# Another order for the opening of a fused attention and Hyena kernel: fp32 loads turned by TensorE, a second batch cast into SBUF, and the filter's spectrum moved into that batch

## The chip, the cores and the metric

The kernel runs on one core of one Trainium2 chip. Time is device time in microseconds (us) for the whole call; most executions of one kernel agree within a few tenths of a per cent.

## The reference

Batch 8, 8 heads, sequence 576, head width 64, 128 random features. The first part is linear attention with cos/sin features, the second a gated FFT convolution.

```python
def phi(x):                                   # attention, per batch and head
    proj = einsum('bhsd,md->bhsm', x, omega)
    return concatenate([cos(proj), sin(proj)], -1) / sqrt(m)
kv  = einsum('bhsm,bhsd->bhmd', phi(k), v);   z = phi(k).sum(axis=2)
num = einsum('bhsm,bhmd->bhsd', phi(q), kv);  den = einsum('bhsm,bhm->bhs', phi(q), z)
x   = (num / den), heads side by side         # (8, 576, 512)
x1, x2, x3 = split(x @ w_proj, 3)             # Hyena part
y   = x1 * irfft(rfft(x2) * rfft(filter_fft)) * x3
out = y @ w_out
```

## The kernel before

For each batch the program issues four `pair(b, hp)` steps of attention (two heads each), interleaved with four `hyena(b - 1, hp)` steps of the batch before. The names matter in the profile: `tk`, `tq` are transposed k and q in PSUM, `kT`, `qT` their copies; `thk`, `thq`, `tht` are projections onto omega; `angk`, `angq`, `angt` angles; `kf`, `qf`, `kft` the cos/sin features; `vh`, `vl` the fp16 high and low parts of v; `kv`, `nd` the attention matmuls; `tx`, `xT` the transposed attention output; `x2p`, `xg` the projections, `yp`, `yg` the spectrum of the input and its product, `xc` the inverse transform, `op` the last projection; `ff` the folded filter and `hps`, `hpi`, `hpm` its spectrum.

```python
def turns(self, th, name):          # one feature: DVE, then GpSimd, then ScalarE's Sin
    t = self.ft.tile([128, 2, w], I32, name=f"ang{name}", tag="ang", bufs=2)
    nc.vector.tensor_scalar(t[:, 0], th, TO_PHASE, None, ALU.mult)
    nc.gpsimd.tensor_scalar(t[:, 1], t[:, 0], 1.0, TURN / 4, ALU.mult, ALU.add)
...
def v_split(self, b, hp):
    nc.scalar.copy(vh, vp)
    nc.gpsimd.tensor_tensor(self.vl[hp], vp, vh, ALU.subtract)
...
def spectrum(self, b):
    self.yg = [mo.tile([128, 2, DM], F32R, name=f"yg{b}_{g}", tag=f"yg{g}") for g in range(2)]
    ...
        nc.gpsimd.tensor_tensor(self.yg[g], t[0], t[1], ALU.add)
...
def run(self):
    self.omega_load()
    self.loads(0)        # k, q of batch 0 cast to fp16 by GpSimd's DMA ring, turned by TensorE
    self.loads(1)        # k, q of batch 1 cast into DRAM, then two DMA transposes (kD -> kT, qD -> qT)
    self.in_weights(); self.buffers()
    self.front(0, 0)
    self.v_split_tails(0)
    for b in range(B + 1):
        for hp in range(4):
            if b < B: self.pair(b, hp)
            if b:     self.hyena(b - 1, hp)
        if b == 0:
            self.filter_spectrum(self.fold_filter())   # fold on DVE, 17 matmuls, 10 evacuations on ScalarE

def pair(self, b, hp):              # front(): k features, v split and q features of the next pair
    if hp < 3: self.front(b, hp + 1)
    elif b + 1 < B: self.front(b + 1, 0)
    ...
    self.kv(b, hp); self.attend(b, hp); ...
```

## Time and profile before

| | before |
|---|---|
| time, median of 3 runs | 432.19 us (431.9 to 434.46) |
| profiled span, mean TensorE clock | 432.9 us, 0.933 |
| busy: PE, DVE, ACT, POOL | 79%, 67%, 55%, 52% |
| x2p of batches 0, 1, 2 starts at | 77.3, 125.6, 173.7 us |

The average shares hide the structure. Up to x2p of batch 0 the core waits for data; from there on each batch takes 47 to 48 us with TensorE dense. (In the timeline x2p of batch 0 starts at 77.27; the chain's entry of 77.49 in the prediction begins where its predecessor ends.)

### The profile page before, as it was taken

The numbers are of one execution on the slowest core, as the hardware profiler recorded it, in microseconds if no ns is written. First come the engines' busy times: TensorE is split into PE (matmuls) and PEld (weight loads), VectorE is DVE, ScalarE is ACT, GpSimd is POOL, SyncE is SP. The second block draws the span as 40 slices with busy tenths as digits, with TensorE's granted clock in tenths as the row PEclk, the third lists the DMA queues.
The fourth block names the chain that finished last, engine by engine and source line by source line (L and its number), as shares of the span: only waits on it lengthen the run. The fifth ranks groups of instructions, "written<-read, shape, count | busy, mean of one in ns | idle before, by whom it ended". The sixth has DMA issues, their size and how long they took to land.

```text
span 432.9 us, 8680 instructions
## 1 busy us (share of the span) xinstructions
PE 340.5 (79%) x3550; PEld 230.4 (53%) x3550; DVE 290.7 (67%) x530; ACT 239.3 (55%) x308; POOL 227.0 (52%) x209
## 2 busy tenths in 40 slices
PE   0277555998779869996989869986899698888982
PEld 0155423666446655565556755666466555673560
DVE  3256963597946888497849786688849784863640
ACT  4056834845766448833884458644883388222432
POOL 7076711378632946477545855294637453423360
PEclk9999956899889989999799969998999979999998
DMA  9999999205940197109930595019510002001203
GB/s 206 204 206 204 286 246 175 49 3 58 235 143 6 10 167 222 43 2 119 226 95 2 62 182 183 14 11 176 108 38 2 2 28 83 2 2 51 59 2 109
DMA packets 76152, 43.50 MB, mean 100 GB/s; under 512 B 43473, under 2 KB 69585, under 8 KB 76113
## 3 DMA queue, kind: packets, MB, share of 16 engines
q1 hardware_dynamic: 52608, 30.52, 30.0%
q0 software_dynamic: 23504, 12.44, 21.5%
q8 instruction: 28, 0.46, 0.5%
q14 instruction: 12, 0.09, 0.1%
HBM read 36.80 MB, written 17.69 MB: 126 GB/s over the span
## 4 chain that ended last, share of the span: by engine, by line
PE 44%; DMA 13%; ACT 12%; DVE 12%; POOL 9%; issue 7%; SPq 2%; POOLq 0%; ACTq 0%; DVEq 0%
PE xg L112 9%; PE kv L420 7%; DMA f<-in_moe_filter_fft_dram 6%; PE xc L112 6%; PE op L112 5%; PE x2p L112 5%; ACT qf L404 4%; ACT kf L382 3%; PE yp L112 3%; DMA out_dram<-o 3%; DMA qa<-in_q_dram 3%; POOL yT L523 3%; PE nd L437 3%; DVE tc L484 3%; ACT o L536 2%
## 5 line engine op out<-in xcount | busy, mean ns | idle before, releaser
L404 ACT ACTIVATE qf<-angq 128x1728 f16<-128x1728 int16 (+1 forms) x48 | 70.4, 1480 | 28.4 <-PE nd L437 20.5
L382 ACT ACTIVATE kf<-angk 128x2048 f16<-128x2048 int16 x32 | 61.1, 1910 | 20.9 <-POOL angk L347 19.0
L112 PE MATMUL xg<-xT,wp 128*128 128x288 f16 x512 | 71.4, 286 | 1.0 <-DVE tc L484 0.3
L347 POOL TENSOR_SCALAR angk<-angk 128x1024 int32<-128x1024 int32 x32 | 33.5, 1046 | 64.7 <-DVE angk L346 64.0
L346 DVE TENSOR_SCALAR angq<-thq 128x864 int32<-128x864 f32 (+1 forms) x48 | 45.6, 952 | 31.4 <-ACT qf L404 20.3
L347 POOL TENSOR_SCALAR angq<-angq 128x864 int32<-128x864 int32 (+1 forms) x48 | 43.2, 900 | 34.5 <-DVE angq L346 33.9
L112 PEld LDWEIGHTS <-wp 128*128 128x128 f16 x512 | 49.3, 98 | 20.2 <-issue 4.2
L485 POOL TENSOR_TENSOR yg<-tc,tc 128x1024 fp32r<-128x1024 f32 x16 | 37.4, 2359 | 36.9 <-DVE tc L484 36.9
L523 POOL TENSOR_TENSOR yT<-w,cv 128x576 f16<-128x576 f32 x32 | 45.7, 1436 | 20.3 <-DVE cv L522 13.2
L503 DVE TENSOR_TENSOR w<-xg,w 128x288 f32<-128x288 f32 x64 | 27.7, 452 | 36.3 <-ACT w L501 18.5
L333 POOL TENSOR_TENSOR vl<-vf,vh 128x512 f16<-128x512 f32 x32 | 36.9, 1155 | 26.7 <-ACT vh L332 26.6
L420 PEld LDWEIGHTS <-kf 128*128 128x128 f16 x1024 | 44.0, 101 | 9.7 <-issue 5.5
L501 ACT ACTIVATE w<-xg 128x288 f32<-128x288 f32 x64 | 24.4, 406 | 38.5 <-PE xg L112 37.9
L112 PE MATMUL op<-wo,yT 128*128 128x512 f16 (+1 forms) x160 | 40.6, 390 | 3.4 <-POOL yT L523 3.4
L346 DVE TENSOR_SCALAR angk<-thk 128x1024 int32<-128x1024 f32 x32 | 39.0, 1218 | 6.3 <-ACT qf L404 5.3
L112 PE MATMUL x2p<-wp,eo 128*128 128x512 f16 x160 | 38.1, 395 | 5.1 <-ACT o L536 4.4
L420 PE MATMUL kv<-vh,kf 128*128 128x65 f16 x512 | 38.8, 199 | 3.6 <-ACT kf L382 1.9
L437 PE MATMUL nd<-kvz,qf 128*128 128x65 f16 x640 | 27.5, 200 | 16.3 <-DVE kvz L425 14.6
L112 PE MATMUL xc<-inv,yg 128*128 128x288 f32 x128 | 35.2, 368 | 5.4 <-ACT w L501 4.6
L437 PEld LDWEIGHTS <-qf 128*128 128x128 f16 x640 | 25.5, 102 | 23.4 <-issue 16.9
L420 PE MATMUL kv<-vl,kf 128*128 128x64 f16 x512 | 37.3, 197 | 0.0
L402 PE MATMUL thq<-qT,om 128*128 128x512 f16 (+1 forms) x96 | 28.4, 378 | 10.9 <-DVE angk L346 6.1
(88 smaller groups left out, 639.6 us busy)
## 6 DMA issues: line engine op xcount, KB each, us to landing
vf<-in_v_dram SPq DMA_DIRECT2D x8, 1024.0 KB, 7.2
qD<-in_q_dram POOLq DMA_DIRECT2D x7, 576.0 KB, 8.7
kD<-in_k_dram POOLq DMA_DIRECT2D x7, 512.0 KB, 6.1
out_dram<-o SPq DMA_DIRECT2D x8, 256.0 KB, 3.0
out_dram<-o SPq DMA_DIRECT2D x8, 224.0 KB, 2.4
wp<-in_moe_w_proj_dram POOLq DMA_DIRECT2D x1, 1536.0 KB, 23.2
out_dram<-o SPq DMA_DIRECT2D x8, 192.0 KB, 3.2
out_dram<-o SPq DMA_DIRECT2D x8, 160.0 KB, 2.1
```

The source lines that it names most:

```text
L112: nc.tensor.matmul(outap, l, r, start=(i == 0), stop=(i == n - 1))
L333: nc.gpsimd.tensor_tensor(self.vl[hp], vp, vh, ALU.subtract)
L346: self.nc.vector.tensor_scalar(t[:, 0], th, TO_PHASE, None, ALU.mult)
L347: self.pool_mark = self.nc.gpsimd.tensor_scalar(t[:, 1], t[:, 0], 1.0, TURN / 4, ALU.mult, ALU.add)
L382: self.marks["k", b, hp] = nc.scalar.activation(kf.rearrange("p t a r m -> p t (a r m)"), ang, AF.Sin, scale=TO_ANGLE)
L402: nc.tensor.matmul(th[:, lo:hi], self.om2[:, r], qT[:, lo:hi], start=True, stop=True)
L404: nc.scalar.activation(self.qf[b][:, :, h0 : h0 + n, r], ang.rearrange("p t (h j) -> p t h j", h=n), AF.Sin, scale=TO_ANGLE,)
L420: nc.tensor.matmul(ps[:, hh, t, : 1 + D] if i < 5 else ps[:, hh, t, :D], l, r_, start=(i == 0), stop=(i == len(terms) - 1),)
L437: nc.tensor.matmul(ps[:, c], qfh[:, t, SOFF[c] : SOFF[c] + 128], kvz[:, hh, t], start=(t == 0), stop=(t == 1),)
L485: nc.gpsimd.tensor_tensor(self.yg[g], t[0], t[1], ALU.add)
L503: nc.vector.tensor_tensor(w[:, ns], ps, w[:, ns], ALU.mult)
L523: nc.gpsimd.tensor_tensor(self.yT[b][:, dc], self.w.pop((b, dc)).rearrange("p a s -> p (a s)"), cv.rearrange("p c z i -> p (c z i)"), ALU. ...
```

## The change

Its intent is to get the first batches going earlier. Batch 0's k, q and v come as plain fp32 through one ring, in the order of use, and TensorE transposes them in fp32. Batch 1's k and q are cast straight into SBUF, into the buffers that `yg` uses later, and TensorE turns them, instead of the way through DRAM. The filter loads no longer wait, and its fold and spectrum move from between batches 0 and 1 into batch 1's loop. (Two smaller parts are not in the cut below: the last filter tile gets other buffers, and the fold is held behind the last attention step of batch 0 instead of the one before.)

```diff
     def run(self):
...
         self.omega_load()
-        self.loads(0)
-        self.loads(1)
-        self.in_weights()
+        self.first_loads()                 # k, q, v of batch 0: nc.sync, FP32, in order of use
         self.buffers()
         self.front(0, 0)
+        with self.tc.issue_after(self.pool_marks["k", 0, 0].ins):
+            self.second_loads()            # k, q of batch 1: nc.gpsimd, cast to FP16 in SBUF
+            self.v_loads(1)
         self.v_split_tails(0)
         for b in range(B + 1):
             for hp in range(4):
                 if b < B:
                     self.pair(b, hp)
+                if b == 1 and hp == 0:
+                    self.fold_filter()
+                if b == 1 and hp == 1:
+                    self.filter_spectrum()
                 if b:
                     self.hyena(b - 1, hp)
-            if b == 0:
-                self.filter_spectrum(self.fold_filter())
...
+    def second_loads(self):
+        ka = mo.tile([128, H, 4 * D], FP16, name="ka1", tag="yg0")
+        qa = mo.tile([128, H, 4 * D], FP16, name="qa1", tag="yg1")
...
     def k_features(self, b, hp):
...
-        if b == 0:
-            self.first_k(blocks, [...], f"tk{hp}")
+        if b < 2:
+            self.first_k(b, hp)
...
-        self.late(nc.sync.dma_start(self.fwd, dr_fwd.ap()), self.marks["k", 0, 1])
+        nc.sync.dma_start(self.fwd, dr_fwd.ap())
...
-                    ld = nc.sync.dma_start(f[p + at : p + at + m], every4[BLOCKS[blk], i : i + m])
-                    self.late(ld, self.marks["k", 0, 1])
+                    nc.sync.dma_start(f[p + at : p + at + m], every4[BLOCKS[blk], i : i + m])
```

More of the change, by code (lines that the diff above doesn't have):

```diff
@@ L39 @@
 QW = 4 * S
-FTAG = ["tc0", "tc1", "tc1", "tc0", "tc0"]
+FTAG = [("tc0", 2), ("tc1", 2), ("tc1", 2), ("tc0", 2), ("xT", 2)]
 QGROUPS = [(0, 3), (3, 3), (6, 2)]
@@ L143, in omega_load @@
         nc, cst = self.nc, self.cst
-        ident = nc.inline_tensor(np.eye(128, dtype=np.float16), name="identc")
+        ident = nc.inline_tensor(np.eye(128, dtype=np.float32), name="identc")
+        self.ident32 = self.mo.tile([128, 128], FP32, name="ident32", tag="cv", bufs=2)
+        nc.sync.dma_start(self.ident32, ident.ap())
+        om = self.mo.tile([128, 64], FP32, name="om", tag="osb", bufs=2)
+        nc.sync.dma_start(om, self.omega)
         self.ident = cst.tile([128, 128], FP16, name="ident", tag="ident")
-        nc.sync.dma_start(self.ident, ident.ap())
-        om16 = cst.tile([128, 64], FP16, name="om16", tag="om16")
-        nc.gpsimd.dma_start(om16, self.omega)
+        nc.vector.tensor_copy(self.ident, self.ident32)
         self.om2 = cst.tile([128, 2, 128], FP16, name="om2", tag="om2")
         nc.vector.memset(self.om2, 0.0)
-        ps = self.bank([128, 128], "omps", FP16)
-        nc.tensor.transpose(ps[:64, :128], om16, self.ident)
+        ps = self.bank([128, 128], "omps")
+        nc.tensor.transpose(ps[:64, :128], om, self.ident32)
         nc.vector.tensor_copy(self.om2[:64, 0], ps[:64, :128])
@@ L174, in weights @@
         with self.tc.issue_after(self.pool_marks["k", 0, 1].ins):
+            self.in_weights()
             nc.gpsimd.dma_start(self.inv, dr_inv.ap())
@@ L191, in filter_loads @@
         for c in range(NC):
-            f = mo.tile([128, 2, DM], FP32, name=f"f{c}", tag=FTAG[c], bufs=2)
+            f = mo.tile([128, 2, DM], FP32, name=f"f{c}", tag=FTAG[c][0], bufs=FTAG[c][1])
             for p, _, lo, n in _filter_rows(c):
                 for blk, i, m, at in _pieces(lo, n, EB):
-                    ld = nc.sync.dma_start(f[p + at : p + at + m], every4[BLOCKS[blk], i : i + m])
-                    self.late(ld, self.marks["k", 0, 1])
+                    nc.sync.dma_start(f[p + at : p + at + m], every4[BLOCKS[blk], i : i + m])
             self.fl.append(f)
@@ L200, in fold_filter @@
         nc, mo = self.nc, self.mo
-        ff = mo.tile([128, NC, DM], FP16, name="ff", tag="x2")
-        with self.tc.issue_after(self.marks["strip", 0, 2].ins):
+        self.ff = ff = mo.tile([128, NC, DM], FP16, name="ff", tag="yT")
+        with self.tc.issue_after(self.marks["strip", 0, 3].ins):
             nc.vector.memset(ff[:, 2], 0.0)
@@ L209, in fold_filter, with filter_spectrum @@
                     )
-        return ff
-    def filter_spectrum(self, ff):
-        nc, cst, fwd = self.nc, self.cst, self.fwd
+    def filter_spectrum(self):
+        nc, cst, fwd, ff = self.nc, self.cst, self.fwd, self.ff
         self.hre = [cst.tile([128, 2, DM], FP16, name=f"hre{g}", tag=f"hre{g}") for g in range(2)]
@@ L249, in loads, with v_tiles @@
     def loads(self, b):
-        nc, raw = self.nc, self.raw
+        self.v_loads(b)
+        self.turned_loads(b)
+    def v_tiles(self, b):
+        raw = self.raw
         vf = raw.tile([128, H, 4, D], FP32, name=f"vf{b}", tag="vf", bufs=2)
@@ L253, in loads @@
         self.vf[b] = vf, vft
-        nc.sync.dma_start(
-            vf.rearrange("p h r d -> p h (r d)"),
-            self.v[b, :, :512, :].rearrange("h (p r) d -> p h (r d)", r=4),
-        )
-        self.tails(nc.sync, vft, self.v, b)
-        self.kT[b] = raw.tile([128, 18, 128], FP16, name=f"kT{b}", tag="kT")
-        self.qT[b] = raw.tile([128, 2 * H, QB], FP16, name=f"qT{b}", tag="qT")
-        if b == 0:
-            self.first_loads()
-        else:
-            self.turned_loads(b)
+        return vf, vft
@@ new lines, in v_loads, with turned_tiles, fours @@
+    def v_loads(self, b, eng=None):
+        nc = self.nc
+        vf, vft = self.v_tiles(b)
+        nc.sync.dma_start(vf.rearrange("p h r d -> p h (r d)"), self.fours(self.v, b, 0, H))
+        self.tails(nc.sync, vft, self.v, b)
+    def turned_tiles(self, b):
+        self.kT[b] = self.raw.tile([128, 18, 128], FP16, name=f"kT{b}", tag="kT")
+        self.qT[b] = self.raw.tile([128, 2 * H, QB], FP16, name=f"qT{b}", tag="qT")
+    def fours(self, src, b, h0, n):
+        return src[b, h0 : h0 + n, :512, :].rearrange("h (p r) d -> p h (r d)", r=4)
@@ L266, in first_loads @@
     def first_loads(self):
         nc, mo = self.nc, self.mo
-        self.ktl = mo.tile([128, 4, D], FP16, name="ktl", tag="od", bufs=2)
-        self.ka = mo.tile([128, H, 4 * D], FP16, name="ka", tag="tc0", bufs=2)
-        self.qa = mo.tile([128, H, 4 * D], FP16, name="qa", tag="tc1", bufs=2)
-        self.qta = mo.tile([128, 4 * D], FP16, name="qta", tag="od", bufs=2)
-        self.tails(nc.gpsimd, self.ktl, self.k, 0)
-        nc.gpsimd.dma_start(self.ka, self.k[0, :, :512, :].rearrange("h (p r) d -> p h (r d)", r=4))
@@ L275, in first_loads @@
-        nc.gpsimd.dma_start(self.qta, self.q[0, :, 512:, :].rearrange("h (i r) d -> h i (r d)", r=4))
-        nc.gpsimd.dma_start(self.qa, self.q[0, :, :512, :].rearrange("h (p r) d -> p h (r d)", r=4))
+        self.turned_tiles(0)
+        vf, vft = self.v_tiles(0)
+        ktl = mo.tile([128, 4, D], FP32, name="ktl0", tag="od", bufs=2)
+        qta = mo.tile([128, 4 * D], FP32, name="qta0", tag="od", bufs=2)
+        ka = [mo.tile([128, 4, 4 * D], FP32, name=f"ka0_{i}", tag="tc0", bufs=2) for i in range(2)]
@@ new lines, in first_loads @@
+        qa = [mo.tile([128, 4, 4 * D], FP32, name=f"qa0_{i}", tag="tc1", bufs=2) for i in range(2)]
+        self.first[0] = (
+            ktl.rearrange("p j d -> p (j d)"), qta,
+            [ka[h // 4][:, h % 4] for h in range(H)], [qa[h // 4][:, h % 4] for h in range(H)],
+            self.ident32, FP32,
+        )
+        for i in range(2):
+            h0 = 4 * i
+            nc.sync.dma_start(ka[i], self.fours(self.k, 0, h0, 4))
+            if i == 0:
+                self.tails(nc.sync, ktl, self.k, 0)
+                nc.sync.dma_start(qta, self.q[0, :, 512:, :].rearrange("h (i r) d -> h i (r d)", r=4))
+            nc.sync.dma_start(qa[i], self.fours(self.q, 0, h0, 4))
+            if i == 0:
+                self.tails(nc.sync, vft, self.v, 0)
+            nc.sync.dma_start(
+                vf[:, h0 : h0 + 4].rearrange("p h r d -> p h (r d)"), self.fours(self.v, 0, h0, 4)
+            )
@@ new lines, in second_loads @@
+    def second_loads(self):
+        nc, mo = self.nc, self.mo
+        self.turned_tiles(1)
+        ktl = mo.tile([128, 4, D], FP16, name="ktl1", tag="osb", bufs=2)
+        qta = mo.tile([128, 4 * D], FP16, name="qta1", tag="ymix")
+        ka = mo.tile([128, H, 4 * D], FP16, name="ka1", tag="yg0")
+        qa = mo.tile([128, H, 4 * D], FP16, name="qa1", tag="yg1")
+        self.first[1] = (
+            ktl.rearrange("p j d -> p (j d)"), qta,
+            [ka[:, h] for h in range(H)], [qa[:, h] for h in range(H)], self.ident, FP16,
+        )
+        self.tails(nc.gpsimd, ktl, self.k, 1)
+        nc.gpsimd.dma_start(ka, self.fours(self.k, 1, 0, H))
+        nc.gpsimd.dma_start(qta, self.q[1, :, 512:, :].rearrange("h (i r) d -> h i (r d)", r=4))
+        nc.gpsimd.dma_start(qa, self.fours(self.q, 1, 0, H))
@@ L278, in turned_loads @@
     def turned_loads(self, b):
         nc = self.nc
+        self.turned_tiles(b)
         kD = self.dram.tile([128, 18 * 128], FP16, name=f"kD{b}", tag="kD")
@@ L296, in turned_loads, with turn @@
         nc.sync.dma_start_transpose(out=self.qT[b], in_=qD)
-    def first_k(self, blocks, srcs, name):
-        nc = self.nc
-        tp = self.bank([128, len(srcs), 128], name, FP16)
+    def turn(self, b, srcs, name):
+        ident, dtype = self.first[b][4:]
+        tp = self.bank([128, len(srcs), 128], name, dtype)
         for j, src in enumerate(srcs):
-            nc.tensor.transpose(tp[:, j], src, self.ident)
-        nc.vector.tensor_copy(self.kT[0][:, blocks], tp)
-    def first_q(self, h0, n):
-        nc, qT = self.nc, self.qT[0]
-        if h0 == 0:
-            tp = self.bank([128, 2, 128], "tqt", FP16)
-            for c in range(2):
-                nc.tensor.transpose(tp[:, c], self.qta[:, 128 * c : 128 * (c + 1)], self.ident)
-            nc.vector.tensor_copy(
-                qT.rearrange("p (h c) i -> p c h i", c=2)[:, :, :, 128:],
+            self.nc.tensor.transpose(tp[:, j], src, ident)
+        return tp
@@ new lines, in evacuate, with first_k, first_k_tails @@
+    def evacuate(self, b, out, tp):
+        if b == 0:
+            self.nc.vector.tensor_copy(out, tp)
+        else:
+            self.nc.scalar.copy(out, tp)
+    def first_k(self, b, hp):
+        ka = self.first[b][2]
+        tp = self.turn(
+            b, [ka[2 * hp + j // 2][:, 128 * (j % 2) : 128 * (j % 2 + 1)] for j in range(4)], f"tk{b}_{hp}"
+        )
+        self.evacuate(b, self.kT[b][:, 4 * hp : 4 * hp + 4], tp)
+    def first_k_tails(self, b):
+        ktl = self.first[b][0]
+        self.evacuate(b, self.kT[b][:, 16:18], self.turn(b, [ktl[:, :128], ktl[:, 128:]], f"tkt{b}"))
@@ L313, in first_q @@
+    def first_q(self, b, h0, n):
+        qT, (_, qta, _, qa) = self.qT[b], self.first[b][:4]
+        if h0 == 0:
+            tp = self.turn(b, [qta[:, :128], qta[:, 128:]], f"tqt{b}")
+            self.evacuate(
+                b, qT.rearrange("p (h c) i -> p c h i", c=2)[:, :, :, 128:],
                 tp.rearrange("p c (h i) -> p c h i", h=H),
             )
-        for h in range(h0, h0 + n):
-            tp = self.bank([128, 2, 128], f"tq{h}", FP16)
-            for c in range(2):
-                nc.tensor.transpose(tp[:, c], self.qa[:, h, 128 * c : 128 * (c + 1)], self.ident)
-            nc.vector.tensor_copy(qT[:, 2 * h : 2 * h + 2, :128], tp)
+        for h in range(h0, h0 + n, 2):
+            m = min(2, h0 + n - h)
+            tp = self.turn(
+                b, [qa[h + j // 2][:, 128 * (j % 2) : 128 * (j % 2 + 1)] for j in range(2 * m)], f"tq{b}_{h}"
+            )
+            self.evacuate(b, qT[:, 2 * h : 2 * (h + m), :128], tp)
@@ L352, in k_tail_features @@
         self.kft[b] = self.ft.tile([128, 2, 4, 128], FP16, name=f"kft{b}", tag="kft")
-        if b == 0:
-            ktl = self.ktl.rearrange("p j d -> p (j d)")
-            self.first_k(slice(16, 18), [ktl[:, :128], ktl[:, 128:]], "tkt")
+        if b < 2:
+            self.first_k_tails(b)
         th = self.pt.tile([128, 512], FP32, name=f"tht{b}", tag="th")
@@ L369, in k_features @@
         blocks = slice(4 * hp, 4 * hp + 4)
-        if b == 0:
-            self.first_k(
-                blocks,
-                [self.ka[:, 2 * hp + j // 2, 128 * (j % 2) : 128 * (j % 2 + 1)] for j in range(4)], f"tk{hp}",
-            )
+        if b < 2:
+            self.first_k(b, hp)
         kT = self.kT[b][:, blocks]
@@ L393, in q_features @@
             self.qf[b] = self.ft.tile([128, 2, H, 2, HS], FP16, name=f"qf{b}", tag="qf", bufs=1)
-        if b == 0:
-            self.first_q(h0, n)
+        if b < 2:
+            self.first_q(b, h0, n)
         qT = self.qT[b][:, 2 * h0 : 2 * (h0 + n)].rearrange("p a i -> p (a i)")
@@ L540, in run @@
     def run(self):
-        for name in ("vf", "kT", "qT", "kf", "kft", "qf", "kvz", "xsd", "xT", "w", "yT", "marks", "pool_marks"):
+        for name in ("vf", "kT", "qT", "kf", "kft", "qf", "kvz", "xsd", "xT", "w", "yT", "marks", "pool_marks",
+                     "first"):
             setattr(self, name, {})
@@ L554, in run @@
                     self.pair(b, hp)
+                if b == 1 and hp == 0:
+                    self.fold_filter()
+                if b == 1 and hp == 1:
+                    self.filter_spectrum()
                 if b:
                     self.hyena(b - 1, hp)
-            if b == 0:
-                self.filter_spectrum(self.fold_filter())
     def pair(self, b, hp):
```

## The prediction

> **What bounds the kernel now.** I read the page's slices first, then the chain that ended last, then windows cut at the points that the chain names.
>
> ```profile
> PE   0277555998779869996989869986899698888982
> PEclk9999956899889989999799969998999979999998
> DMA  9999999205940197109930595019510002001203
> ```
>
> A slice is 10.8 us. For the first seven (to 75 us) the DMA row is full while PE is far from it; afterwards PE stays at 8 or 9 with DMA half idle. So there are two regimes: a start that waits for data, and a steady state in which TensorE is nearly dense. The chain of waits (start, us, what) gives the dates:
>
> ```profile
> 4.80 13.31 DMA qa<-in_q_dram
> ...
> 44.45 13.22 DMA f<-in_moe_filter_fft_dram
> 57.69 0.98 SPq L195
> 58.72 14.11 DMA f<-in_moe_filter_fft_dram
> ...
> 77.49 4.72 PE x2p L112 x20
> ...
> 125.58 6.18 PE x2p L112 x20
> ...
> 173.68 1.04 PE x2p L112 x4
> ```
>
> Two data waits are on it: q of batch 0 (to 18.1) and the filter (44.4 to 72.8). x2p is the first matmul of a batch's second half (the hyena part). Batch 0's starts at 77.5, batch 1's 48.1 us later, batch 2's 48.1 after that; the page's later ones follow at 47. The stretches between (from:to and length, then busy us and instructions of PE, its weight loads, DVE, ACT and POOL, then granted clock, DMA share, GB/s):
>
> ```profile
> 50.00:60.00 10.00, 3.91 (x15) 1.70 (x15) 8.31 (x16) 5.08 (x3) 5.61 (x7) 0.71 1.13 199
> 60.00:70.00 10.00, 7.16 (x55) 3.42 (x54) 3.69 (x6) 5.92 (x7) 1.92 (x2) 0.60 1.13 240
> 70.00:77.50 7.50, 3.83 (x30) 2.56 (x30) 4.57 (x6) 3.20 (x6) 0.91 (x1) 0.59 1.03 168
> 77.50:125.60 48.10, 40.31 (x442) 27.37 (x441) 38.67 (x69) 31.19 (x39) 30.03 (x27) 0.96 0.47 93
> 125.60:173.70 48.10, 41.55 (x438) 27.97 (x438) 35.30 (x63) 28.87 (x38) 28.03 (x25) 0.93 0.52 100
> ```
>
> From 50 to 77 PE does only 100 matmuls, at 0.6 to 0.7 of its clock; in the steady batches it is busy 40 to 41.5 of 48 us, the most of any engine. Three lines of the timeline date the attention of batch 0:
>
> ```profile
> 22.47 1.91 ACT L382 ACTIVATE kf<-angk 128x2048 f16<-128x2048 int16 x1 [0.96 <-POOL angk L347]
> 56.60 0.46 DVE L457 COPY xT<-tx 128x576 f16<-128x576 f16 x1 [0.83 <-PE tx L456]
> 72.93 0.69 DVE L207 TENSOR_TENSOR ff<-f 128x512 f16<-128x512 f32 x1 [6.78 <-DMA f<-in_moe_filter_fft_dram]
> ```
>
> Attention takes 34.1 us from its first k features to its last xT copy (22.5 to 56.6); x2p follows only 20.9 us later, because the filter's last piece arrives at 72.8 and everything on DVE and PE queues behind its fold. The compiled order of the changed kernel is, on PE, the same as before for the last 2853 matmuls, from batch 2 on. So the change can only move the date of x2p of batches 0, 1 and 2; what is gained there is gained at the end.
>
> **What the Trainium skill says.** "DMA: Bandwidth & Descriptors", section Queues, rings and completion order: each DMA engine takes turns between the queues that have work, so a load in one ring is slowed by loads in another. Two more windows (the last column is GB/s written) agree that what shares the rings matters:
>
> ```profile
> 4.00:6.00 2.00, 0.00 (x0) 0.00 (x0) 0.00 (x0) 0.00 (x0) 2.00 (x4) 1.00 1.07 323
> 16.00:20.00 4.00, 1.86 (x15) 1.59 (x14) 0.80 (x2) 0.00 (x0) 0.20 (x1) 1.00 1.55 191
> ```
>
> At 4 to 6 us mostly plain fp32 v moves, at 16 to 20 us only casts, which read twice what they write.
>
> "TensorE: Matmul & The Clock Gate", Part 4: PE-mode transpose, says a transpose ends in PSUM and needs a copy out, and does not count as activity that releases the clock gate. Before, PE runs its first 128-wide matmuls slowly (four thk of 256 columns in 1.0 us at 19 us, 0.6 us at 95 us), so PE is cold there and I expect it to stay so. For fp32 the pages pull apart: the same page's Terms call fp32 transpose mode "4× faster", while "FP8 and Floating Point Precision", TensorE Precision Notes, counts four passes for true fp32. No run here has an fp32 transpose; I take 0.43 us each (an estimate: four times the 0.107 us per cold 128-column matmul that follows from those thk, less 0.2 us for the last one's latency as one kv shows it) as the dear end. "VectorE: DVE Perf Modes", Why PSUM operands drop a tier: fp32 out of PSUM runs at 1×. The trace has 0.42 us for an fp16 copy of 512 columns and 0.69 for 512 columns of fp32 angt; I use 0.6 to 0.7.
>
> **The change part by part.** It removes batch 1's detour through DRAM (casts there, two DMA transposes back), the marks that held fwd and filter back until the second k features, and the spectrum of the filter from between batches 0 and 1; it moves that spectrum into batch 1, and batch 1's transposes to PE.
>
> Loads of batch 0. One ring, fp32: identity 64 KB, omega 32, k heads 0-3 512, k tails 128, q tails 128, q 512, v tails 128, v 512, then 512 each of k, q, v: 3.55 MB. At about 300 GB/s (below the 323 above) from 2.3 us: first k at 4.5 to 5.3, k tails 6, q 8, all at 14.5 to 15. Nothing else is in the rings then: the casts of batch 1 queue on GpSimd behind its first angk (about 12). Then 6 fp32 transposes (2.6), copy (0.6), thk (1.0), angt and angk on DVE (about 2.2 with a copy), angk on GpSimd (1.04): first k features at about 12.5 instead of 22.5. Gain 10.
>
> Attention of batch 0. Removed from its stretch: nothing large; the 4.4 us block of four vl on GpSimd is now interleaved. Added: DVE fp32 copies, about 1.5 us in sum; GpSimd issues of batch 1's casts, wp, inv and wo, some 6 us; PE up to 30 x 0.32 = 10 us of longer transposes, a third of it on the path; ScalarE copies of batch 1's transposes, 4 us; and ScalarE's order now holds vh of batch 1, which must wait for kv of pair 1, ahead of q features of group 1. I keep 34.1 and add 1.5: last xT at about 48.
>
> From there to x2p. The fold's 6 adds and a memset (6 x 0.68 + 0.27 = 4.4 us) still lie on DVE ahead of eo, now with batch 1's angk (1.2), two angq (2.1), kvz, rd, xsd (1.8) and eo (1.5) in the queue: 11 us of DVE. ScalarE's side (two qf 3.3, three copies 1.6, kf 1.9, with the two angle buffers between) comes out at the same. Less 0.5 for eo's second half: x2p of batch 0 at 58 instead of 77.5. Gain 19.5. The filter must have landed by then. Behind the 3.55 MB come v of batch 1 (1.18 MB), fwd (0.98) and filter (2.36) in one ring, k, q (1.18) and wp (1.57) in the other: 7.3 MB at about 220 GB/s (mean of the windows before 75 us, 191 to 323) is 33 us, done at about 48. It is covered, narrowly. So are the buffers: the filter's third and fourth tiles wait for the last transposes of q and k, at about 32.
>
> Batch 1, x2p to x2p. It was 48.1 us with PE dense, and gets PE work: the filter spectrum's 17 matmuls of 512 columns at 0.22 (warm, x2p: 20 in 4.72) 3.7; transposes of k pairs 2, 3 and q group 2, 12 at about 0.08, 1.0; thk of pairs 2 and 3, which before ran in the shadow of the filter wait, 0.8. ScalarE's 10 evacuations of the spectrum (0.6 each, 6 us) hold the four PSUM banks: 1 to 2 us of PE stall. Sum 7: 55 us. x2p of batch 1 at 58 + 55 = 113 instead of 125.6. Gain 12.6, and it stays to the end: 432.2 - 12.6 = 419.6.
>
> **The rivals.**
> 1. DMA stays the bound: the load order only shifts bytes, and batch 0 carries 1.18 MB more than with casts. For it: the DMA row is full to 75 us. Against: two transposes through DRAM (k and q of batch 1) are gone, and all that must land before x2p is 10.8 MB. If the filter or wp landed at 65, x2p would start at 66 and the end be about 428.
> 2. The work given back in batch 1 eats more than 7: yg now shares buffers with batch 1's k and q, so GpSimd's yg waits for the last transposes and holds angk of pair 3; ScalarE carries 13 more operations. PE has about 7 us of idle in the stretch to absorb part, or the stalls add 5: end at 424 to 426, inside 2%.
> 3. The fp32 transposes are cheap and PE gets warm early: attention shrinks to 31 us, x2p at 53, the end at about 413.
> 4. DMA transposes of batch 2 come late, as kD of batch 2 queues behind wp, inv and wo on one ring: thk of batch 2 would wait at about 80 us. I estimate its arrival at 75; a miss costs 2 to 4.
>
> **Range and chances.** The two large terms have errors of about 5 (date of x2p) and 4 (length of batch 1), together 6 to 7: 419.5, from 410 to 428. The 2% line is at 423.5; 0.6 of such an error below it: faster 0.72. Slower by 2% would need both terms to fail wholly: 0.02.
>
> **What would show it.** In the changed profile: q of batch 0 gone from the chain, first kf near 12.5, last xT near 48, no filter wait of over 2 us on DVE, x2p at 58, 113 and then every 47 us; PE clock low until about 40 us only. The prediction is wrong if the chain still shows a DMA wait for f or wp, if an fp32 transpose takes much less or more than 0.1 to 0.43 us, or if batch 1 needs over 60 us.

## More of the kernel before

Spans and dates inside a kernel come from one profiled execution each, and single executions of one kernel differ by 1 to 6 us here, so dates are used to see *where* time moved and timed runs to say *how much*.

## The result, and the profile after

The changed kernel takes 438.69 us in the median of 4 runs (438.05 to 439.25) against 433.03 us for the kernel before in the same rounds (431.9 to 434.46). The ratio is 1.0128, 95% interval 1.0089 to 1.0168. A ratio here is always the mean time of one kernel's runs over that of the other's in the same rounds, so it is not quite the ratio of the medians. The change loses 1.3% where a gain of 3% was forecast; the result is within 2%, but outside the predicted range of 410 to 428.

The slices of the changed kernel (one slice is now 10.9 us):

```profile
PE   3655628877769868896899869986999698888981
PEclk9897868999678999999699979999999979999996
DMA  7999995004970098208930495019410003001203
```

TensorE works from the first slice on, and the DMA row is full to the end of the sixth slice instead of the seventh: the opening did get shorter. But slices 8 to 12 of PE stand at 8, 7, 7, 7 and 6, where the kernel before had 9, 9, 8, 7 and 7.

Three lines of the timeline (start, duration, engine, line, operation) answer to the three dates that the prediction named:

```profile
13.14 1.91 ACT L435 ACTIVATE kf<-angk 128x2048 f16<-128x2048 int16 x1 [0.96 <-POOL angk L404]
50.67 0.46 DVE L510 COPY xT<-tx 128x576 f16<-128x576 f16 x1 [0.18 <-PE tx L509]
62.70 0.65 DVE L209 TENSOR_TENSOR ff<-f 128x512 f16<-128x512 f32 x1
```

The first k features come at 13.1 instead of 22.5. Batch 0's attention ends at 51.1 instead of 57.1. The last fold waits for no DMA any more. The chain of waits (start, us, what) shows what took the place of the filter:

```profile
17.75 16.02 DMA f<-in_moe_filter_fft_dram
...
34.20 22.10 DMA vf<-in_v_dram
56.38 0.63 ACT vh L389
57.01 0.07 issue
57.08 1.12 POOL vl L390
58.20 1.46 POOL angk L404
59.68 1.92 ACT kf L435
...
64.78 6.31 PE x2p L112 x20
```

x2p of batch 0 is at 64.8, a gain of 12.5 us on 77.3. What ends last before it is the load of **v of batch 2**: data of a batch that is not needed for another 60 us. It delays x2p by way of GpSimd: `vl`, which needs `vh`, stands there ahead of the angles (`angk`) of batch 1's second k features (`kf`). The windows from there on (length, then busy us of PE, weight loads, DVE, ACT, POOL, then granted clock, DMA share, GB/s):

```profile
60.00:64.78 4.78, 0.00 (x1) 0.01 (x1) 3.16 (x6) 3.75 (x3) 1.88 (x2) 0.50 0.95 156
64.78:128.73 63.95, 48.95 (x478) 32.08 (x479) 40.19 (x67) 36.96 (x50) 29.99 (x27) 0.90 0.46 94
128.73:176.97 48.24, 40.72 (x438) 26.71 (x438) 36.38 (x64) 29.46 (x39) 26.90 (x24) 0.95 0.54 103
```

From x2p of batch 0 to x2p of batch 1 it now takes 63.9 us instead of 48.3; the next batch is back at 48.2. So the sum in the profiled spans is -12.5 for the opening, +15.6 for batch 1 and about +1 for the rest: 437.1 against 432.9. In batch 1 PE is busy 48.95 us against 40.5 before, and idle 15.0 against 7.8: about half of the growth is work and half is waiting. A part of the work is clock: PE is idle for 7.5 us ahead of x2p (the first window above shows the last 4.8 of them), and x2p's 20 matmuls then take 6.31 us, the first 3.7 of them at clock 0.50, against 4.72 before. The Trainium skill ("TensorE: Matmul & The Clock Gate", Part 1) says that the clock comes back after about 4 us of sustained matmuls. The trace agrees: in windows of 2 us the clock is 0.50 until 68 us and 1.00 from 69 us on.

### The profile page after: what moved, and what is told of

Its sections match the earlier page's. It is cut to its first block, busy times and chain, and to the rows that moved or that the text cites. A ratio compares the mean times of both kernels' runs of the same rounds, so it can differ in the third digit from the quotient of the medians.

```text
span 437.1 us, 8777 instructions
## 1 busy us (share of the span) xinstructions
PE 340.9 (78%) x3586; PEld 232.5 (53%) x3586; DVE 295.9 (68%) x528; ACT 243.0 (56%) x318; POOL 224.5 (51%) x204
## 4 chain that ended last, share of the span: by engine, by line
PE 42%; ACT 14%; DVE 12%; DMA 11%; POOL 9%; issue 7%; SPq 4%; POOLq 0%; ACTq 0%; DVEq 0%
PE xg L112 9%; PE kv L473 6%; PE xc L112 6%; PE x2p L112 5%; DMA vf<-in_v_dram 5%; PE op L112 5%; ACT kf L435 4%; DMA f<-in_moe_filter_fft_dram 4%; ACT qf L457 4%; PE yp L112 3%; POOL yT L576 3%; PE nd L490 2%; DMA out_dram<-o 2%; POOL angk L404 2%; ACT o L589 2%
## 5 line engine op out<-in xcount | busy, mean ns | idle before, releaser
L112 PE MATMUL x2p<-wp,eo 128*128 128x512 f16 x160 | 40.1, 409 | 11.2 <-DVE eo L518 7.5
L554 ACT ACTIVATE w<-xg 128x288 f32<-128x288 f32 x64 | 24.6, 406 | 38.3 <-PE xg L112 37.5
L490 PEld LDWEIGHTS <-qf 128*128 128x128 f16 x640 | 24.6, 99 | 30.8 <-issue 24.1
L589 ACT ACTIVATE o<-op 128x512 f32<-128x512 f32 (+1 forms) x40 | 22.9, 593 | 22.0 <-PE op L112 12.2
```

Source lines behind the costliest of these rows:

```text
L112: nc.tensor.matmul(outap, l, r, start=(i == 0), stop=(i == n - 1))
L490: nc.tensor.matmul(ps[:, c], qfh[:, t, SOFF[c] : SOFF[c] + 128], kvz[:, hh, t], start=(t == 0), stop=(t == 1),)
L589: nc.scalar.mul(o[:n], ps[:n], 1.0 / YS)
```

## The experiments

There were three calls of 4, 4 and 3 kernels, each timed against the kernel before in its own rounds; all results were correct. The dates are of the profiled run of each. A difference against the changed kernel compares medians of different calls, in which the kernel before moved between 432.2 and 433.4 us, so it is good to about 1 us; the dates carry the 1 to 6 us of single executions, so small differences between them are readings.

| kernel | time, median us | ratio to before (95%) | x2p of batch 0 | batch 1, x2p to x2p |
|---|---|---|---|---|
| before | 432.2 to 433.4 | 1 | 77.3 | 48.3 |
| changed | 438.69 | 1.0128 (1.0089 to 1.0168) | 64.8 | 63.9 |
| late_vh | 435.97 | 1.0056 (1.0001 to 1.0112) | 62.1 | 64.5 |
| between | 431.67 | 0.9966 (0.9905 to 1.0026) | 63.9 | 58.1 |
| dram1 | 427.47 | 0.9870 (0.9818 to 0.9922) | 65.0 | 53.5 |
| early_turns | 430.39 | 0.9943 (0.9874 to 1.0012) | 64.8 | 54.0 |
| own_tail | 437.04 | 1.0104 (1.0060 to 1.0148) | 66.1 | 62.0 |
| cast0 | 439.18 | 1.0141 (1.0096 to 1.0187) | 68.1 | 63.5 |
| late_btw_early | 426.18 | 0.9849 (0.9795 to 0.9904) | 64.7 | 52.8 |
| all3 | 428.26 | 0.9901 (0.9841 to 0.9961) | 68.8 | 49.1 |
| late_early | 427.50 | 0.9861 (0.9827 to 0.9895) | 64.8 | 55.0 |
| late_dram | 427.14 | 0.9865 (0.9830 to 0.9899) | 64.6 | 55.0 |
| dram_between | 428.65 | 0.9901 (0.9859 to 0.9942) | 70.0 | 51.9 |

Each diff is against the changed kernel.

### late_vh: the split of v of batch 2 behind batch 1's second k features

```diff
+        if (b, hp) == (2, 0):
+            with self.tc.issue_after(self.marks["k", 1, 1].ins):
+                nc.scalar.copy(vh, vp)
+            with self.tc.issue_after(self.pool_marks["k", 1, 1].ins):
+                nc.gpsimd.tensor_tensor(self.vl[hp], vp, vh, ALU.subtract)
+            return
```

> The changed kernel with ScalarE's and GpSimd's split of v of batch 2, pair 0, placed behind the second k features of batch 1 instead of ahead of them. Theory A (ScalarE's wait for v of batch 2, 3.8 us, sets the date of x2p of batch 0): x2p of batch 0 moves from 64.8 to about 61, the end from 438.7 to about 435. Theory B (something else, the fold or eo on DVE or the filter, would hold x2p to the same date): x2p moves by less than 1 us and the end by less than 1.

First the changed kernel, on ScalarE (ACT) and GpSimd (POOL), then ScalarE in this one (in brackets the idle time before, and what ended it):

```profile
56.38 0.62 ACT L389 CAST vh<-vf 128x512 f16<-128x512 f32 x1 [3.79 <-DMA vf<-in_v_dram]
57.08 1.12 POOL L390 TENSOR_TENSOR vl<-vf,vh 128x512 f16<-128x512 f32 x1 [5.40 <-ACT vh L389]
58.17 1.48 POOL L404 TENSOR_SCALAR angk<-angk 128x1024 int32<-128x1024 int32 x1
59.68 1.91 ACT L435 ACTIVATE kf<-angk 128x2048 f16<-128x2048 int16 x1 [2.68 <-POOL angk L404]
```

```profile
56.27 1.91 ACT L441 ACTIVATE kf<-angk 128x2048 f16<-128x2048 int16 x1 [3.90 <-POOL angk L410]
...
59.62 0.60 ACT L391 CAST vh<-vf 128x512 f16<-128x512 f32 x1
```

The features come 3.4 us earlier, x2p of batch 0 at 62.1 (2.7 earlier), and the timed median is 2.7 us lower. The wait for v of batch 2 therefore cost 2.7 us. It is real but explains only 2.7 of the 6.8 us by which the date was missed, 64.8 against 58. (The edit moves the halves on ScalarE and on GpSimd together. In the changed kernel `kf` waits for GpSimd's `angk`, and that stands behind `vl`: by the trace the delay runs over both engines, and no run moves one half alone.)

### between: fold and spectrum back between batches 0 and 1

```diff
-                if b == 1 and hp == 0:
-                    self.fold_filter()
-                if b == 1 and hp == 1:
-                    self.filter_spectrum()
                 if b:
                     self.hyena(b - 1, hp)
+            if b == 0:
+                self.fold_filter()
+                self.filter_spectrum()
```

> The changed kernel with the fold and the filter spectrum back between batch 0 and batch 1; everything else as changed. Theory A (inside batch 1 the spectrum costs far more than its 3.7 us of matmuls, since ScalarE's ten evacuations and the late features stand in the path): x2p of batch 0 comes 3 to 5 us later than 64.8, x2p to x2p of batch 1 falls from 64 to 56, the end to about 435. Theory B (it costs the same wherever it stands): the two dates shift against each other and the end stays within 1 us of 438.7.

Putting the spectrum in front of x2p of batch 0 did not delay x2p: it started at 63.9, 0.9 earlier. ScalarE's first evacuation and its next v split in this kernel:

```profile
54.44 0.59 ACT L222 CAST hre<-hps 128x512 f16<-128x512 f32 x1 [3.46 <-PE hps L112]
...
61.70 0.62 ACT L389 CAST vh<-vf 128x512 f16<-128x512 f32 x1 [1.01 <-PE kv L473]
```

The spectrum's ten evacuations (54.4 to 59.4) fall into a stretch in which ScalarE of the changed kernel was mostly idle, for 3.79 us until v came and for 2.68 until the angles behind it were made. Batch 1 shrinks by 5.8 us, and the time by 7.0. So the move of the spectrum gained nothing in front of x2p and cost about 6 us behind it.

### dram1: batch 1's k and q through DRAM again

```diff
-        if b < 2:
+        if b == 0:
             self.first_k(b, hp)            # likewise first_k_tails and first_q
...
-            self.second_loads()
+            self.turned_loads(1)
```

> The changed kernel with batch 1's k and q again cast into DRAM and turned by DMA (issued where the changed kernel issues its casts). Theory A (batch 1's transposes on PE, their copies on ScalarE and the yg buffers they occupy cost some 5 to 6 us): last xT of batch 0 comes 2 to 3 us earlier than 51.1, batch 1 shrinks from 64 to about 60, the end is about 433. Theory B (the DMA path now is the late one: the transposes stand ahead of fwd and filter in the one ring): x2p of batch 0 is not earlier than 64.8 because the filter lands at 55 or later, and the end is 438 or more.

Batch 1 takes 53.5 us instead of 63.9 and the time falls by 11.2 us, to below the kernel before. x2p of batch 0 stays at 65.0, although v of batch 2 no longer delays it (its split waits on ScalarE from 60 to 68 us, behind the features that x2p needs). In place of that wait came a later attention: batch 1's k arrives through the DMA transpose at 42.3, the last xT of batch 0 comes at 54.5 instead of 51.1, and DVE, idle for no more than 0.4 us between 50 and 66 us, reaches the six adds of the fold at 59.7 and `eo` behind them. This run says that casting batch 1 into SBUF and turning it on TensorE costs 10 us in batch 1, but not yet why.

### early_turns: the last turns of batch 1 ahead of its pair 2

```diff
-        if b < 2:
+        if b == 0 or (b == 1 and hp < 3):
             self.first_k(b, hp)
+        if b == 1 and hp == 2:
+            self.first_k(1, 3)
+            self.first_q(1, 6, 2)
...
-        if b < 2:
+        if b == 0 or (b == 1 and g < 2):
             self.first_q(b, h0, n)
```

> The changed kernel with the last transposes of batch 1 (k pair 3, q group 2) done together with those of k pair 2, so that yg's buffers are free before yg is due. Theory A (yg waits for these transposes and holds the angles of pair 3 behind it on GpSimd): yg starts at about 86 instead of 89.2, kf of pair 3 about 6 us earlier than 94.9, batch 1 shrinks by 3 to 4, the end is about 435. Theory B (the late features are hidden behind the dense PE): the end stays within 1 us of 438.7.

The same transposes and copies are done on the same engines, only earlier, ahead of the filter's spectrum. x2p of batch 0 stays at 64.8, batch 1 shrinks from 63.9 to 54.0 in the profiled run (the fastest of the four, 428.46), and the median falls by 8.3 us. So most of dram1's gain (9.9 of 10.4 us in the profile, 8.3 of 11.2 in the median) is had without taking the work of turning away; it is the *place* of the last turns that costs. GpSimd's timeline of the changed kernel, beside it two lines of GpSimd in this experiment:

```profile
89.19 4.67 POOL L538 TENSOR_TENSOR yg<-tc,tc 128x1024 fp32r<-128x1024 f32 x2 [11.26 <-PE tk L343]
93.81 1.05 POOL L404 TENSOR_SCALAR angk<-angk 128x1024 int32<-128x1024 int32 x1
```

```profile
77.80 1.05 POOL L404 TENSOR_SCALAR angk<-angk 128x1024 int32<-128x1024 int32 x1
...
84.40 4.70 POOL L541 TENSOR_TENSOR yg<-tc,tc 128x1024 fp32r<-128x1024 f32 x2 [4.16 <-DVE tc L540]
```

In the changed kernel the turn of k of pair 3 (`tk` at 88.7) stands on TensorE behind the whole filter spectrum and batch 0's `yp`. GpSimd sits idle for 11.3 us until that turn frees `yg`'s buffer, then adds `yg` for 4.7 us, and only then, at 93.8, makes the angles of pair 3; its features follow at 94.9. Without the wait for `yg` they could have come about 2 us sooner, for DVE had made its half of these angles by 91.7; the rest of the delay is that the turn comes so late. In the experiment the angles are made at 77.8, ahead of `yg`, and the features come at 83.4. (The edit changes the order on TensorE, ScalarE and GpSimd together; own_tail below takes one of these apart.) The kernel before had angles ahead of `yg` too:

```profile
80.22 1.04 POOL L347 TENSOR_SCALAR angk<-angk 128x1024 int32<-128x1024 int32 x1 [1.11 <-DVE angk L346]
...
90.84 4.67 POOL L485 TENSOR_TENSOR yg<-tc,tc 128x1024 fp32r<-128x1024 f32 x2 [2.71 <-DVE tc L484]
```

### own_tail: the shared buffer alone

The last heads of batch 1's k and q (6 and 7) get buffers of their own, so that `yg` no longer waits for their turns, which stay where they are.

```diff
-        ka = mo.tile([128, H, 4 * D], FP16, name="ka1", tag="yg0")
+        ka = mo.tile([128, 6, 4 * D], FP16, name="ka1", tag="yg0")
+        kz = mo.tile([128, 2, 4 * D], FP16, name="ka1z", tag="ka1z")
...                                          # the same for q, and two loads each
```

> The changed kernel with heads 6 and 7 of batch 1's k and q in two small buffers of their own, so that yg no longer waits for the last transposes; the transposes and the order of GpSimd's instructions (yg ahead of the angles of pair 3) stay. Theory A (the wait for yg's buffers itself is the cost that early_turns took away): yg at about 86.5, batch 1 from 64 to 56 or less, the end near 430. Theory B (the cost is that the features of pair 3 and group 2 come late and behind yg on GpSimd, whoever waits): yg earlier by 2.7, batch 1 shorter by 3 at most, the end 435 to 437.

`yg` now starts 1.8 us earlier, waiting only for its operands, but batch 1 shrinks by no more than 1.9 us (62.0) and the time by 1.7, with overlapping intervals. The buffer that rival 2 of the prediction named is thus a small part. The rest of the 10 us goes with the late place of the turns. Even here the angles of pair 3 come at 93.6, and by the trace it is not `yg` that holds them: GpSimd is done with `yg` and idle for 1.56 us until DVE's half of the angles arrives, and that waits for the turn (`tk` at 90.5) and `thk` (91.6) on TensorE:

```profile
87.37 4.67 POOL L543 TENSOR_TENSOR yg<-tc,tc 128x1024 fp32r<-128x1024 f32 x2 [7.66 <-DVE tc L542]
93.61 1.04 POOL L409 TENSOR_SCALAR angk<-angk 128x1024 int32<-128x1024 int32 x1 [1.56 <-DVE angk L408]
```

### cast0: batch 0 by casts again

```diff
-        ka = [mo.tile([128, 4, 4 * D], FP32, name=f"ka0_{i}", ...
+        ka = [mo.tile([128, 4, 4 * D], FP16, name=f"ka0_{i}", ...
...
-            nc.sync.dma_start(ka[i], self.fours(self.k, 0, h0, 4))
+            nc.gpsimd.dma_start(ka[i], self.fours(self.k, 0, h0, 4))   # same for q and the tails
```

> The changed kernel with batch 0's k and q cast by GpSimd's ring into fp16 and turned as fp16, in the same pieces and order. Theory A (the fp32 ring is what brings the first features to 13.1): first k features at 15 to 17, last xT of batch 0 2 to 3 later than 51.1, the end 441. Theory B (the order of use and the later casts of batch 1 bring it, not the type): first k features within 1.5 us of 13.1, last xT and the end within 1.

The first k features come at 16.4 instead of 13.1 and x2p of batch 0 at 68.1 instead of 64.8. These 3.3 us are not all due to the type: GpSimd's angles for these features are ready only 0.8 us later (13.9 instead of 13.1), and the rest is spent on ScalarE, where the compiler now placed four `vh`, which wait for v until 12.95, ahead of the features, with a table load behind them. The timed medians differ by only 0.5 us, which the intervals do not separate. The profiled run was the slowest of its four (441.4), so part of the 3.3 us may belong to that execution; how much of a gain at x2p of batch 0 arrives at the end, this run does not show.

### late_btw_early: three mends together

The edit is late_vh, between and early_turns in one kernel.

> The changed kernel with the three repairs that moved it, together: split of v of batch 2 later, spectrum between the batches, last transposes of batch 1 earlier. If the three costs are separate (2.9 at x2p of batch 0, 5.8 and 9.9 in batch 1): x2p of batch 0 at about 61.5, batch 1 about 48 to 50, the end 419 to 422, faster than before by 2.5 to 3 percent. If they are the same stall seen three times: batch 1 at 54, the end 426.

At 426.18 us it is the fastest median, 1.5% below the kernel before, but the mends do not add up. x2p of batch 0 is at 64.7: with v out of the way, the spectrum in front of x2p, its ten evacuations ending at 60.3 us, sets the date instead. Batch 1 takes 52.8 us.

### all3: late_vh, between and dram1 together

> The changed kernel with batch 1 again through DRAM, the spectrum between the batches and the split of v of batch 2 later: of the change only batch 0's fp32 ring and the order of the loads remain. If the filter's landing (in one ring behind batch 1's DMA transposes) bounds it: x2p of batch 0 at 65 to 67, batch 1 48, the end 424 to 427. If not: x2p of batch 0 at 61, the end 420.

Batch 1 is back to 49.1 us, the least of all variants. But x2p of batch 0 is at 68.8, because the last filter piece is folded at 61.8 and the spectrum follows it in front of x2p. 428.26 us is no better than dram1.

### late_early: late_vh and early_turns

> The changed kernel with two mends: vh and vl of batch 2, pair 0, after k features (1,1), and batch 1's last turns (k pair 3, q group 2) in front of its pair 2. If the two measured costs are separate (2.7 us at x2p of batch 0, 9.9 us in batch 1), x2p of batch 0 is at 62, batch 1 takes 54, and the profiled span is about 424, the time about 427.5. If they overlap, as three mends did before, x2p comes at 62 but batch 1 takes 56 or more and the time stays at 430, that of early_turns alone.

The time of 427.50 us is what the sum of the two effects gives: 2.7 and 8.3 us off 438.69 are 427.7. The profile shows x2p at 64.8, not at 62. In the profiled run TensorE waited for the cast of batch 1's q (the bracket is the idle time and what ended it), a wait that the changed kernel's profile does not have; these turns start at 42.9 instead of 41.0, which accounts for about 2 of the 2.7 us.

```profile
42.91 0.82 PE L343 MATMUL tq<-ident,qa 128*128 128x128 f16 x6 [1.67 <-DMA qa<-in_q_dram]
```

Whether this load comes late in most runs is not known from one profile.

### late_dram: late_vh and dram1

> The changed kernel with batch 1's k and q through DRAM as before, and vh and vl of batch 2 late; the spectrum stays inside batch 1. With DRAM for batch 1 alone the filter landed at 59.7 and x2p of batch 0 stayed at 65.0. If the filter's landing sets it there, late vh changes nothing: x2p 65, batch 1 53.5, time 427.5. If the wait for v of batch 2 set it there too, x2p is at 62.5 and the time 425.

x2p of batch 0 at 64.6, batch 1 at 55.0 and 427.14 us equal dram1 within its interval. The first branch of the expectation held in its numbers: with batch 1 through DRAM, v of batch 2 sets nothing. Its reason did not: as told under dram1, DVE reaches the fold late (59.7) and then waits for no piece of the filter.

### dram_between: the fp32 ring and the freed filter loads alone

> Only the first of the three parts of the change: batch 0 by one fp32 ring and turned by TensorE; batch 1's k and q through DRAM, and the spectrum between batch 0's attention and its hyena part, as in the kernel before. If what the change lost lies in batch 1 (its turns and the spectrum), batch 1 takes 48 to 50 here; x2p of batch 0 then comes later by what the spectrum takes after the filter's landing at 60: at about 67 to 69, against 77.3 before, and the time is 423 to 425. If the fp32 ring alone brings a cost into batch 1, it takes over 53.

Batch 1 takes 51.9 us, 2 more than expected, and the time is 428.65, some 4 more; the profiled run, at 432.96, was the slowest of the six, so its dates are rough. Still, what is left of the change here (the fp32 ring in order of use, and filter loads that no longer wait) beats the kernel before by 1.0%. cast0, in which the type and ring alone were worth 0.5 us, suggests that the gain lies more in the order than in fp32; no run separates the two here.

Four of the kernels form a square. All have the fp32 ring; they differ in where batch 1's k and q go and where the spectrum stands (ratios to before):

| | spectrum between the batches | spectrum inside batch 1 |
|---|---|---|
| batch 1 through DRAM | 0.9901 (dram_between) | 0.9870 (dram1) |
| batch 1 cast into SBUF | 0.9966 (between) | 1.0128 (changed) |

Moving the spectrum alone is harmless (0.9870 against 0.9901, intervals overlapping), casting batch 1 alone costs 0.7% (intervals overlapping too), and both together cost 2.3%. So most of the loss is an interaction. By the profiles (dram_between's is rough) it has two parts. With batch 1 through DRAM, moving the spectrum brings x2p of batch 0 forward by 5.0 us (70.0 to 65.0) and lengthens batch 1 by 1.6; with batch 1 cast, x2p does not come forward (63.9 to 64.8; late_vh puts 2.7 us of that date down to v of batch 2), and batch 1 grows by 5.8. early_turns (0.9943) shows what lies behind the second part: the spectrum was put in front of turns that the cast had created. With both mends in place it no longer matters where the spectrum stands (late_early 0.9861, late_btw_early 0.9849, intervals overlapping).

## Why the prediction was right or wrong

**Right in the main: the bound of the kernel before and its removal.** DMA set the opening; in the changed kernel q of batch 0 is off the chain, the first k features came at 13.1 (predicted 12.5), the filter landed before it was needed, and no fold waited for a DMA. That 12.5 was met so closely is partly luck: the k tails let TensorE start at 7.5 and not at about 6, and the steps from there to the features took 5.6 us and not the 7.4 of the prediction's sum. Rival 1, DMA staying the bound through the filter or `wp`, did not happen as told; but a load is still on the chain, v of batch 2 queued behind the filter's issues. Rival 4 did not happen: the DMA transpose of batch 2's k was issued at 60.0, and no projection of the changed kernel waited for one.

Two of the prediction's readings need a word. The two windows that it sets beside the page on rings each hold the traffic of one ring (0.63 of 0.65 MB, and all of 0.77 MB), so they show a rate without and with casts and not one ring slowing another. And the clock of 1.00 in its second window is from before the first entry of that trace's clock record (at 37.2 us), so it says nothing against the slow matmuls there.

**Nearly right: attention of batch 0.** Its last xT was predicted to start at 48 and started at 50.7. As for these 2.7 us, the trace shows DVE idle for 3.9 us at 36 to 40, waiting for the k tail projection of batch 1: its transposes and copies stand on PE and ScalarE, ScalarE was behind q features that waited for GpSimd, and GpSimd was in three `vl` in a row, two of them of batch 1. No run took this apart, so it stays a reading. The fp32 transposes, which the prediction priced at up to 0.43 us each, were not the reason: a group of four took 1.06 us at 8 us and 0.60 at 11 us. The clock had come up in between: the first entry of this trace's clock record, at 10.5 us, is a change to full clock, and four `thk` took 0.92 us at 9.8 and 0.61 at 16.2. So the prediction's cold PE "until about 40 us" was wrong and rival 3's premise right (cheap transposes, PE warm early), but not its consequence: attention took 37.5 us from the first features to the last xT, and not 31. Whether transposes alone bring the clock up, no run here shows; projections ran between them.

```profile
7.95 1.06 PE L343 MATMUL tk<-ident,ka 128*128 128x128 f32 x4
...
11.21 0.60 PE L343 MATMUL tk<-ident,ka 128*128 128x128 f32 x4
```

**Wrong, first step: "ScalarE's side ... comes out at the same. ... x2p of batch 0 at 58".** The count of ScalarE's work was of its instructions and left out one wait. In the compiled order the split of v of batch 2 stands ahead of the second k features of batch 1, on ScalarE (`vh`) and on GpSimd (`vl`, ahead of their angles). Its load is issued by SyncE in order behind the twelve pieces of the filter, which themselves waited for buffers; SyncE's longest wait for a filter buffer in the changed kernel between 10 and 60 us (engine, line, what it waited for: us in total, times, longest) is for the transposes of q that free a filter tile, which the prediction had dated but held to be harmless:

```profile
SPq L198 <- PE tq L343: 6.1, 1, 6.1
```

The rest of SyncE's waiting between the filter's pieces, about 7 us, is for earlier loads to land. So v was issued at 34.2, took 22.1 us to land at 56.3, and x2p came at 64.8. late_vh measured the split's place at 2.7 us. Of the 6.8 us miss another 2.7 are the attention above, and about 1.4 no run assigns.

**Wrong, second step: "Batch 1, x2p to x2p ... Sum 7: 55 us".** This is the larger failure: it took 63.9, a growth of 15.6 instead of 7. The mechanism of the sum (spectrum, turns and thk moved into a dense batch) was right as far as it went: the spectrum was put at 3.7 plus 1 to 2 of stall, and `between` gave 5.8. What the sum lacked is that order costs more than work. The turns of k pair 3 and q group 2, priced at a share of 1.0 us, stood behind the spectrum on PE, and so the features of pair 3 came 11.5 us later than with early turns, some 2 us of it because their angles also stood behind `yg` on GpSimd. early_turns measured 9.9 us in batch 1 and 8.3 in the time. Rival 2 had the right place and direction, but named `yg`'s buffer as the cause and gave 5 us to it; own_tail measured that at about 2. With early turns batch 1 takes 54.0, a little under the predicted 55, so the place of the turns is enough to explain the excess. The cold clock of x2p (1.6 us), which the sum did not have either, is in both.

**Wrong in the view of the kernel before.** The prediction took about half of the 20.9 us between attention's end and x2p as idle time to be won, and charged 7 us for the work moved out of it. In that stretch the kernel before also did the spectrum and fronts of batch 1 while the filter came. Shorten the wait, and this work comes due somewhere. The mended variants fit this, though they do not prove it: five of them (dram1, late_early, late_dram, late_btw_early, all3) end at 426 to 428 us, a gain of about 5 us, however early their x2p of batch 0 is (64.6 to 68.8).

**A version that beats both kernels** exists in several forms, at 1.3 to 1.5% below the kernel before: the change with early turns and the late split (427.50), or with batch 1 through DRAM (427.47), or with three mends (426.18). Their intervals overlap, so none is shown to be best. What fixes the floor near 427 us stays open.

## What to carry to other kernels

Before pricing a wait as idle time, list what else runs inside it: work hidden there does not vanish with the wait. When work moves into a dense stage, its cost is set also by what it is placed *in front of* on each engine, so read the compiled order of every engine, the helper engines too, for instructions that wait on late data or stand between a producer and its short consumer. And try the parts of a change apart and in pairs: here two parts that cost under 1% each cost 2.3% together.

## What the Trainium skill lacked or had wrong

- "TensorE: Matmul & The Clock Gate", Terms, calls fp32 transpose mode 4× faster, and "FP8 and Floating Point Precision", TensorE Precision Notes, counts four passes for true fp32; neither gives the cost of an fp32 transpose. Here a group of four fp32 transposes of 128x128 took 0.60 us at 11 us, when the clock was up, the same as four fp16 matmuls of 256 columns (0.60), where four fp16 transposes of that size took 0.39. Less 0.2 us of latency for the last one, that is, by estimate, about 0.10 us each against 0.05, so twice an fp16 one and not four times.
- "DMA: Bandwidth & Descriptors", Queues, rings and completion order, treats the order inside a ring. It gives no measure of what the order in front of a ring costs: SyncE waited 6.1 us for a buffer of one load with all its later loads behind it, and v of batch 2, for which no wait of its own is recorded, was issued only at 34.2 us, directly behind the filter's last piece.
